# A new issue table for a linear-attention and gated-MLP kernel, and a new rule for its filler matmuls

## The chip, the cores and the metric

One Trainium2 chip, of which one core is used. The metric is the device time of one execution in microseconds; runs of the kernel before took 381.42, 377.19 and 382.31 us, median 381.42 us. A page and a trace of one profiled execution, 379.98 us long, stand behind everything that is said of the inside.

## The reference

Two parts follow each other. The first is a recurrent attention over 768 steps for 4 batches and 8 heads of width 48; its output, transposed to (4, 768, 384), is the input of the second, an MLP with a spatial gate.

```python
for t in range(S):
    cur = np.einsum('bhd,bhe->bhde', u[None] * kt, vt)
    y[:, :, t] = np.einsum('bhd,bhde->bhe', rt, state + cur)
    state = wt[:, :, :, None] * state + np.einsum('bhd,bhe->bhde', kt, vt)
...
h = np.maximum(x @ w_in, 0.0)
u, v = (h[..., :d_ff // 2], h[..., d_ff // 2:])
v_n = (v - mu) / np.sqrt(var + 1e-06)
v_s = np.einsum('ts,bsd->btd', w_spatial, v_n) + b_spatial[None, :, None]
gated = u * v_s
return (gated @ w_out).astype(np.float32)
```

## The kernel before

The sequence is cut into chunks of 128 steps, six for each batch, so that 24 *slots* (i = 0 to 23) make up the attention. In a slot, the decays W are multiplied up along time by two scans on VectorE (DVE), F and W; kk and rr (k and r) are multiplied by them on DVE or GpSimd (POOL); TensorE (PE) then forms kk times rr (tile pp, `slot_a`, L487), transposes kk (pt, `slot_kt`, L504), multiplies the transposed KT by v for the state (pp, `slot_pd`, L562), and writes the output py by four strips of 32 rows at a time (`slot_inter` and `slot_intra`, both through `mm_y` at L516). These are small matmuls of 48 or 64 rows and columns. The first six slots get their diagonal from a matmul with two columns (pg, L417), the later ones from a product N on DVE or POOL. DVE copies pp under a mask into As (L490), which `slot_intra` multiplies with v. The state goes through S0 and three tiles SA (`slot_s`).

The MLP works on the attention's output, xT, with each operand split into a high and a low part of a shorter float type; `mm3` (L614 to L616) makes one product as three matmuls. `hv_unit` makes v (ph, 128x512), `scale` normalises it into vh and vl, `g_unit` makes u (pu) and the spatial product (pv, with the spatial weights ws), both 128x384, and multiplies them into gh and gl; `out_unit` makes the output (po), which is copied to ot and stored. Weights are loaded as raw 64-bit words and unpacked on the engines (`split64`, tiles wi and wo; `prep_sp`, tile ws).

All of this is recorded as 1,757 operations (`op`), each with its engines, its cost as the planner sees it, and what it reads and writes. The order is not found while the kernel is built: the string PLAN has for each operation, in the order of recording, an engine letter (T, V, A, G, S for PE, DVE, ScalarE, POOL, SyncE) and a start time in base 36, in hundredths of a microsecond. `plan` sorts the operations by these times, and `issue` writes them in that order to the engines' queues. The times do nothing else to the real operations: each engine takes its queue in order and waits by semaphores for what it needs. All loads and stores go through SP's queue in this order too.

PE's clock has two levels. To keep it up in the first part, where PE has gaps, `fill` goes through the planned order and puts *filler* in gaps ahead of PE operations: calls of one 128x128 matmul of zeros zk into an unused part of pyw (`warm`, L854). It stops at the operation `last`, which is recorded after slot 5 (FILL_TO). In the trace each filler is two instructions, since a product of 32-bit floats is issued in two. After this the page has PE busy to the end.

Of the kernel before, what the change touches and what calls it, by code (L numbers as in the profile page):

```python
# [29 lines left out]
T19r Sdc S9l S4k6 S39x S73 Akk Vmy Vo7 Vu9 A17i G1pt Sc3 Auf Vw8 Vxh V16p A27a G29r Spa A1ek V1hp V1ka V1nn  # L30
A1po G1ut S3c S4l S5u S8c Vfg Tuv Vbj Vf0 Vh4 Vhs Aog Ghl Vl9 Axn Anx Ayb Tla Amp Tol Vq6 Grk Txe Tyf V14x
T17c T18p A1ao T1cf A1di S1f0 A1we V1zy V22k V265 A3bk G3ep Smg A162 V18e V1de V1g1 A1o0 V3lp S1xh A29v V2tt
V2v2 V2zd A36l V3p2 S3vw A4s6 V4x8 S2ic A2tg V4da S1yq A2cw G3y8 S1zz A2e2 V3u9 S450 A58r V5ch S2y9 A3fr
G40w S6e4 A6qj G7n2 S57l A5hr G5rf S6xs A7fr G7ke S218 A2gj G2lj S4vq A5bb V5gc S7wr A85w G87j S1b9 A3d0
V4el V4fo V4hb A4m1 V4o8 S2fu A2x9 V312 V324 V3jg A44m G47p S4ix A4tb V4v8 V4yj V506 A566 V57p S3l3 V3x9
V4im V4jo V4mo A532 V561 T1vz T2fn T2oz A2ro A2uw A2ye Sau Sfu Sel Skj Vz5 T11h Vr3 Vvx Vx5 V11r A159 G11a
G19k A1g0 A1a5 A1go V10u G14q T14z A18y T1at V1ch V1f3 T1gn T1ng V1pk T1s0 T1ux A1xt T1za A20e T21v T2i5
T2k2 A2q1 A2ul A2v9 Snp S10d S1a0 S1ci V1im T1kx V19b V1pc V1rd V1sm A1w3 V1lz V20v A1nq A1sb A21z V1ro G1t8
T1p5 A1r4 T1tm V1vr G1y8 T242 T253 V29i T2by T2db A2f7 T2hl A2io T2qx T2vi T2xg A332 A381 A38p A3b1 V3ch
V3c7 V3ct G3di G3ea G3i4 G3iw A3pt A3t5 V3vk A3nu A417 V45k A3lv A46t V4bm S1dr S1pe S1w8 S1tw V24h T26s  # L40
V1wr V248 V2bb V2ck A2g9 V27u G2g6 A29l A21g A2jq V2bm G2d6 T2aa A2bp T2ec V2fx V2k4 T2m9 T2na V2pf T2t4
# [71 lines left out]
Tqgf Vqh9  # L113
"""

GAP, FILL_TO = 0.8, 5

EARLY = 8

# [872 lines left out]
```

## Time and profile before

| | before |
|---|---|
| runs, median of 3 | 381.42 us (377.19 to 382.31) |
| the profiled execution | 379.98 us |
| its span, first to last instruction | 378.2 us |
| mean granted PE clock, share of full | 0.963 |
| PE matmuls busy, share of the span | 95% |
| DVE, ScalarE (ACT), POOL busy | 67%, 50%, 28% |
| matmul instructions, filler among them | 5994, 48 |

The 1.8 us between the execution's own time and its span lie around the profiled instructions. Busy time of PE is modelled at the ends of its pipelined matmuls. In the clock column 1.00 is 2.4 GHz and 0.50 is 1.2 GHz. "PE" rows are matmuls, "PEld" rows the loads of their weights, which run beside the matmul ahead. Where a wait is put down to "issue", the profile shows nothing that the engine waited for.

### The profile page before, as it was taken

What the parts mean: (1) busy time and instruction counts of PE and PEld (TensorE: products, weight loads), DVE (VectorE), ACT (ScalarE), POOL (GpSimd) and SP (SyncE); (2) the same over time, 40 slices, a digit from 0 to 9 for tenths busy, and PEclk for the clock granted to TensorE, in tenths of its full rate; (3) what the DMA queues carried; (4) which work ended last, traced back from release to release, by engine and by line L of the source; (5) the groups of instructions that cost most, each with busy time, mean ns of one, the idle gap of its engine ahead of it and who ended that gap; (6) DMA issues with size and microseconds to landing.
All of it is one profiled execution on the core that took longest, in us unless ns stands there. A gap on an engine that the chain in (4) does not pass through costs nothing.

```text
span 378.2 us, 13807 instructions
## 1 busy us (share of the span) xinstructions
PE 361.2 (95%) x5994; PEld 327.0 (86%) x5994; DVE 253.4 (67%) x491; ACT 190.4 (50%) x525; POOL 107.0 (28%) x140
## 2 busy tenths in 40 slices
PE   5799899999999999999999999999999999999995
PEld 5777678899889788999988898989989888999995
DVE  6989489999877786867577587656556754342131
ACT  2556578994456437872244138651154336722122
POOL 3505417114314242170401312144620041003111
PEclk9856599999999999999999999999999999999999
DMA  7967447673564645424233637243234420120221
GB/s 207 248 174 221 127 121 234 177 207 105 159 177 118 185 143 167 148 72 156 68 114 92 196 103 223 58 157 85 50 109 146 132 63 5 27 77 2 55 93 66
DMA packets 33023, 47.91 MB, mean 127 GB/s; under 512 B 3264, under 2 KB 21824, under 8 KB 32960
## 3 DMA queue, kind: packets, MB, share of 16 engines
q1 hardware_dynamic: 32960, 47.00, 43.0%
q8 instruction: 48, 0.79, 0.9%
q14 instruction: 15, 0.12, 0.1%
HBM read 42.27 MB, written 4.72 MB: 124 GB/s over the span
## 4 chain that ended last, share of the span: by engine, by line
PE 78%; DMA 8%; DVE 5%; ACT 4%; issue 2%; POOL 2%; SPq 1%; DVEq 0%; POOLq 0%; ACTq 0%
PE pyw L516 9%; PE pv L614 8%; PE pv L615 8%; PE pv L616 8%; PE ph L614 5%; PE ph L616 4%; PE ph L615 4%; PE pu L614 4%; PE po L614 4%; PE po L616 4%; PE po L615 4%; PE pu L615 3%; PE pu L616 3%; DMA kk<-in_tr_dram 3%; PE pp L487 3%; DMA rr<-in_tr_dram 3%
## 5 line engine op out<-in xcount | busy, mean ns | idle before, releaser
L614 PE MATMUL pv<-ws,vh 128*128 128x384 f32 x192 | 66.8, 348 | 0.0
L615 PE MATMUL pv<-ws,vh 128*128 128x384 f32 x192 | 64.9, 338 | 0.6 <-POOL ws L325 0.6
L616 PE MATMUL pv<-ws,vl 128*128 128x384 f32 x192 | 64.8, 338 | 0.0
L720 DVE TENSOR_TENSOR t<-pv,b_sb 128x384 f32<-128x384 f32 x32 | 17.7, 553 | 30.9 <-PE pv L616 30.8
L614 PEld LDWEIGHTS pv<-ws,vh 128*128 128x128 f32 x192 | 36.0, 188 | 1.3 <-ACT ws L323 0.3
L615 PEld LDWEIGHTS pv<-ws,vh 128*128 128x128 f32 x192 | 36.1, 188 | 0.9 <-POOL ws L325 0.9
L616 PEld LDWEIGHTS pv<-ws,vl 128*128 128x128 f32 x192 | 36.1, 188 | 0.0
L724 ACT CAST gh<-t 128x384 fp32r<-128x384 f32 x32 | 15.9, 512 | 38.3 <-POOL t L722 25.6
L614 PE MATMUL pu<-xT,wi 128*128 128x384 f32 x96 | 34.0, 355 | 0.0
L614 PE MATMUL po<-wo,gh 128*128 128x384 f32 x96 | 32.8, 342 | 0.0
L615 PE MATMUL pu<-xT,wi 128*128 128x384 f32 x96 | 32.4, 338 | 0.0
L432 DVE TENSOR_TENSOR_SCAN F<-W,zz 112x512 f32<-112x512 f32 x24 | 29.1, 1212 | 5.0 <-ACT zz L444 3.7
L616 PE MATMUL pu<-xT,wi 128*128 128x384 f32 x96 | 32.4, 337 | 0.0
L615 PE MATMUL po<-wo,gh 128*128 128x384 f32 x96 | 32.3, 336 | 0.0
L616 PE MATMUL po<-wo,gl 128*128 128x384 f32 x96 | 32.3, 336 | 0.0
L614 PE MATMUL ph<-wi,xT 128*128 128x512 f32 x72 | 31.5, 438 | 0.0
L582 POOL TENSOR_TENSOR SA<-S,prod 112x256 f32<-112x256 f32 x22 | 17.5, 797 | 43.9 <-DVE S L579 25.1
L616 PE MATMUL ph<-wi,xT 128*128 128x512 f32 x72 | 29.5, 409 | 0.1
L615 PE MATMUL ph<-wi,xT 128*128 128x512 f32 x72 | 29.3, 407 | 0.0
L442 DVE TENSOR_TENSOR_SCAN W<-W,zz 112x512 f32<-112x512 f32 x24 | 29.1, 1212 | 0.2
L471 ACT ACTIVATE As<-id,dg 128x64 f32<-128x64 f32 x112 | 28.3, 338 | 0.1
L600 ACT CAST xT<-pyw 128x384 fp32r<-128x384 f32 x24 | 11.5, 481 | 32.4 <-PE pyw L516 31.0
(184 smaller groups left out, 817.3 us busy)
## 6 DMA issues: line engine op xcount, KB each, us to landing
N<-in_nat_dram SPq DMA_DIRECT2D x18, 384.0 KB, 3.7
Nw<-in_gt_dram SPq DMA_DIRECT2D x16, 384.0 KB, 3.5
W<-in_tr_dram SPq DMA_DIRECT2D x24, 224.0 KB, 4.1
kk<-in_tr_dram SPq DMA_DIRECT2D x24, 224.0 KB, 3.8
rr<-in_tr_dram SPq DMA_DIRECT2D x24, 224.0 KB, 4.0
v<-in_nat_dram SPq DMA_DIRECT2D x24, 192.0 KB, 3.9
out_dram<-ot SPq DMA_DIRECT2D x24, 192.0 KB, 3.1
wst<-in_w_spT_dram SPq DMA_DIRECT2D x12, 192.0 KB, 4.5
```

The source lines that it names most:

```text
L432: op({"V": 1.22}, lambda: nc.vector.tensor_tensor_scan(flat(F())[:, ::-1], W[:, 2:][:, ::-1], flat(zz[:R])[:, ::-1], 0.0, ALU.mult, ALU.ma ...
L442: op({"V": 1.22}, lambda: nc.vector.tensor_tensor_scan(W[:, :n], W[:, :n], flat(zz[:R]), 0.0, ALU.mult, ALU.max), r=[("zz", 0)], w=[wk])
L471: e.mul(As()[:, h, :], id2, dg()[:, h:h + 1])
L487: nc.tensor.matmul(pa[ts, j, g, :], kk()[rs, g, ts], rr()[rs, g, ts], start=True, stop=True)
L516: nc.tensor.matmul(py[Q * n:Q * (n + 1), x, k_, :], a, b, start=(x, n) not in seen, stop=True, skip_group_check=True)
L582: op({"V": 0.42, "G": 0.617}, lambda e: e.tensor_tensor(new, S0, Wc.unsqueeze(2).broadcast_to([R, G, E2]), ALU.mult), r=[("S0",), ("Wc", i ...
L600: op({"A": 0.48}, lambda: nc.scalar.copy(part(hi), ps), r=[("py", 0)], w=[(hi, j)], banks=("PY",))
L614: nc.tensor.matmul(ps, ah, bh, start=first, stop=False)
L615: nc.tensor.matmul(ps, ah, bl, start=False, stop=False)
L616: nc.tensor.matmul(ps, al, bh, start=False, stop=last)
L720: op({"V": dve(HT)}, lambda: nc.vector.tensor_tensor(t1(), pv()[:, :HT], b_sb[:, tsl], ALU.add), r=[(pv, 0), ("b", 0)], w=[(t1, 0)])
L724: op({"A": act(HT)}, lambda: nc.scalar.copy(gh(), t1()), r=[(t1, 0)], w=[(gh, 0)])
```

## The change

The table PLAN is replaced as a whole; two constants and the filler's rule are new; the planner's costs of six PE operations are written anew. No operation is added or removed but filler, and an operation that may run on several engines may change its engine.

```diff
-T19r Sdc S9l S4k6 S39x S73 Akk Vmy Vo7 Vu9 A17i G1pt Sc3 Auf Vw8 Vxh V16p A27a G29r Spa A1ek V1hp V1ka V1nn
...
+T2vp S9l Sau S3tl S3cw Sjh A1ae V1e8 V1fh V1i2 A1n6 V1z1 S8c Asu Vvj Vws Vys A18y V1nj Swg A1eb V1h5 V1ko
...
-GAP, FILL_TO = 0.8, 5
+GAP, FILL_TO = 0.35, 5
+
+WINDOW, DUTY = 3.41, 0.7
...
-        op({"T": 0.32}, tp, r=[(kk, 0)], w=[(pm_, 0)])
+        op({"T": 0.36}, tp, r=[(kk, 0)], w=[(pm_, 0)])
...
-        op({"T": 0.28}, mm, r=[(rr, 0)] + [("SA", (2 * i + x) % NA) for x in range(first, 2)],
+        op({"T": 0.33}, mm, r=[(rr, 0)] + [("SA", (2 * i + x) % NA) for x in range(first, 2)],
...
-        op({"T": 0.49}, mm, r=[(As, 0), (v, 0), ("vp", i % 2)], w=[("py", 0)], mode="strips", banks=("PY",))
+        op({"T": 0.62}, mm, r=[(As, 0), (v, 0), ("vp", i % 2)], w=[("py", 0)], mode="strips", banks=("PY",))
...
-            op({"T": 0.694}, lambda k_=k_: mm3(
+            op({"T": 0.70}, lambda k_=k_: mm3(
...
-            op({"T": 0.523}, lambda k_=k_: (us(), mm3(
+            op({"T": 0.53}, lambda k_=k_: (us(), mm3(
...
     def fill(order):
-        t = first = 1.1
+        t, runs = 1.9, []
+
+        def busy(a, b):
+            return sum(max(0.0, min(e, b) - max(s, a)) for s, e in runs)
+
         for o in order:
             if o.on == "T":
-                if t < last.start and o.start - t > GAP:
-
-                    warm((o.start - t - GAP) / (0.214 if t > first else 0.43))
-                t = max(t, o.start + o.eng["T"])
+                s, took = o.start, o.eng["T"]
+                if t < last.start:
+                    n = int(min((DUTY * WINDOW - busy(s - WINDOW, s)) / 0.214 + 0.99, (s - t - GAP) / 0.214))
+                    if n > 0:
+                        warm(n)
+                        runs.append((t, t + n * 0.214))
+                runs.append((s, s + 0.85 * took))
+                t = max(t, s + took)
             yield o
```

The other two products of 128x384 go from 0.523 to 0.53 in the same way. The old rule fills every planned gap of more than 0.8 us up to 0.8 us. The new one looks, ahead of each PE operation, at the planned time just before it, counts filler in full and every other PE operation at 85% of its planned length, and puts in as many fillers as bring the share to 0.7, as far as the planned gap less 0.35 us has room. The program has 24 fillers before and 39 after.

PE's queue at its start, up to slot 1's diagonal (pg); pyw<-zk is filler, pt, pp and pg belong to slot 0 first. Before:

```order
L854 MATMUL pyw<-zk 128x128 x13
L504 MATMUL pt_188<-ident,kk_145 128x112 x4
L562 MATMUL pp<-v_151,KT_195 48x48 x16
L854 MATMUL pyw<-zk 128x128 x5
L417 MATMUL pg_232<-up_sb,rk_163 128x2 x4
L516 MATMUL pyw<-rr_147,SA_126 32x64 x8
L487 MATMUL pp<-rr_147,kk_145 64x64 x16
L417 MATMUL pg_282<-up_sb,rk_276 128x2 x4
```

After:

```order
L856 MATMUL pyw<-zk 128x128 x12
L506 MATMUL pt_186<-ident,kk_147 128x112 x4
L419 MATMUL pg_193<-up_sb,rk_166 128x2 x4
L856 MATMUL pyw<-zk 128x128 x2
L564 MATMUL pp<-v_156,KT_198 48x48 x16
L856 MATMUL pyw<-zk 128x128 x6
L518 MATMUL pyw<-rr_145,SA_126 32x64 x8
L489 MATMUL pp<-rr_145,kk_147 64x64 x16
L419 MATMUL pg_276<-up_sb,rk_242 128x2 x4
```

Slot 0's diagonal pg goes ahead of the state product, and there are two groups of filler after it instead of one ahead of it.

PE's queue right behind this, from slot 1's transpose to the first strips of slot 1 (rr_160 before, rr_154 after). Before:

```order
L504 MATMUL pt_290<-ident,kk_165 128x112 x4
L516 MATMUL pyw<-As_251,vp_121 32x64 x16
L516 MATMUL pyw<-As_251,v_151 32x64 x16
L516 MATMUL pyw<-rr_147,SA_126 32x64 x8
L854 MATMUL pyw<-zk 128x128
L562 MATMUL pp<-v_170,KT_341 48x48 x16
L604 MATMUL pyw<-xT_0_0_350,nident 128x192 x2
L854 MATMUL pyw<-zk 128x128 x2
L516 MATMUL pyw<-rr_160,SA_125 32x64
```

After:

```order
L506 MATMUL pt_290<-ident,kk_160 128x112 x4
L518 MATMUL pyw<-As_230,vp_121 32x64 x16
L518 MATMUL pyw<-As_230,v_156 32x64 x16
L518 MATMUL pyw<-rr_145,SA_126 32x64 x8
L856 MATMUL pyw<-zk 128x128 x2
L564 MATMUL pp<-v_206,KT_334 48x48 x16
L606 MATMUL pyw<-xT_0_0_350,nident 128x192 x2
L856 MATMUL pyw<-zk 128x128 x8
L518 MATMUL pyw<-rr_154,SA_125 32x64
```

The real work stands in the same order; there are 2 and 8 fillers where there were 1 and 2. Behind the pp matmuls of slot 1 the new queue has another 6 ahead of its As matmuls, where the old one has 2 ahead of slot 2's pg.

SP's queue around the load of kk for slot 17 (kk17; the number behind a name is the slot's, W0 and W1 are the two tiles of W, out_0_dram a store of the output). Before:

```order
L380 DMA W1_116<-in_tr_dram 112x4x128
L387 DMA N17_3460<-in_nat_dram 128x768
L384 DMA rr16_3468<-in_tr_dram 112x512
L380 DMA W0_115<-in_tr_dram 112x4x128
L742 DMA out_0_dram<-ot0_1_2_2722 128x384
L384 DMA kk17_3566<-in_tr_dram 112x512
L388 DMA v17_3571<-in_nat_dram 128x384
```

After:

```order
L382 DMA W1_116<-in_tr_dram 112x4x128
L399 DMA Nw9_3456<-in_gt_dram 128x768
L386 DMA kk17_3464<-in_tr_dram 112x512
L386 DMA rr16_3470<-in_tr_dram 112x512
L744 DMA out_0_dram<-ot1_0_2_3549 128x384
L386 DMA rr17_3560<-in_tr_dram 112x512
L382 DMA W0_115<-in_tr_dram 112x4x128
```

kk17 has moved ahead of rr16, of the load of W0 and of the store that stood just before it.

## Rows read from the trace of the kernel before

**Rows 1.** The page's busy us (share of the span) and instructions of each engine

```profile
span 378.2 us, 13807 instructions
...
PE 361.2 (95%) x5994; PEld 327.0 (86%) x5994; DVE 253.4 (67%) x491; ACT 190.4 (50%) x525; POOL 107.0 (28%) x140
```

**Rows 2.** Stretches: length, busy us of each engine (instructions), granted clock, DMA share, GB/s

```profile
0.00:16.00 16.00, 10.09 (x133) 9.24 (x134) 12.55 (x27) 5.92 (x17) 5.87 (x21) 1.00 0.89 229
16.00:33.00 17.00, 16.43 (x342) 13.84 (x343) 14.88 (x23) 8.78 (x26) 7.29 (x7) 0.50 0.63 170
33.00:36.40 3.40, 3.11 (x76) 2.13 (x75) 3.40 (x7) 3.27 (x13) 0.30 (x2) 0.99 1.00 297
36.40:46.60 10.20, 8.43 (x164) 6.41 (x172) 5.39 (x10) 5.53 (x19) 5.31 (x5) 0.50 0.57 166
46.60:77.00 30.40, 29.21 (x672) 24.36 (x657) 27.82 (x54) 25.70 (x70) 9.92 (x10) 1.00 0.63 177
77.00:378.00 301.00, 293.90 (x4633) 271.00 (x4631) 189.38 (x375) 141.23 (x385) 78.34 (x98) 1.00 0.38 111
```

**Rows 3.** PE's waits up to 47 us: releaser, us in total, times, longest

```profile
PE pyw L854 <- DVE pyw L269: 1.9, 1, 1.9
PE pyw L516 <- issue: 1.7, 1, 1.7
PE pt L504 <- POOL kk L445: 1.6, 1, 1.6
PE pg L417 <- DVE e_('wv', 0)_172 L352: 1.3, 1, 1.3
...
PE pt L504 <- ACT dg L459: 0.3, 1, 0.3
```

**Rows 4.** Timeline of PE: like work at half and full clock (start, us, instructions)

```profile
10.13 1.38 PE L854 MATMUL pyw<-zk 128*128 128x128 f32 x10
...
23.81 1.22 PE L854 MATMUL pyw<-zk 128*128 128x128 f32 x4
...
26.46 1.14 PE L487 MATMUL pp<-rr,kk 48*64 48x64 f32 x32
27.52 1.01 PE L504 MATMUL pt<-ident,kk 112*128 112x112 f32 x4
...
31.65 0.63 PE L615 MATMUL ph<-wi,xT 128*128 128x512 f32 x1
...
46.81 0.69 PE L487 MATMUL pp<-rr,kk 48*64 48x64 f32 x32
...
47.77 0.39 PE L615 MATMUL ph<-wi,xT 128*128 128x512 f32 x1
...
51.98 0.55 PE L504 MATMUL pt<-ident,kk 112*128 112x112 f32 x4
```

**Rows 5.** Waits of PE's weight loads from 77 us on

```profile
PEld pyw L516 <- issue: 5.9, 22, 0.4
PEld pyw L516 <- DVE As L490: 2.3, 4, 1.0
...
PEld pv L615 <- POOL ws L325: 0.9, 1, 0.9
...
PEld pp L562 <- DVE vl L686: 0.3, 1, 0.3
```

**Rows 6.** The chain that ended last, around slot 17's kk (start, us, what)

```profile
209.48 0.84 SPq L742
...
210.44 4.45 DMA kk<-in_tr_dram
...
214.91 0.70 DVE kk L445
...
215.75 0.57 PE pt L504 x4
```

More of the change, by code (lines that the diff above doesn't have):

```diff
@@ new lines @@
+T2xr V312 T34b T361 A38c T3bq A3do T3g9 T3i7 T3k5 A3pl A3rl A3s9 S24g S2gj S2nu S2va G308 T3cg V2pc V2zr
+V32u V343 A3d8 G340 V37l A3gd A3u8 A3ka V336 G3ff T38s A3c1 T3ey V3ic V3lh T3p7 T3qe V3t7 T3wg T3y6 A40j
+T43m A45x T4j0 T4ky T4mw A4rc A4td A4u0 S2u1 S2zp S37h S3bn V3jt T3mp V3f7 V3mf V3vy V3wk A425 V3nz V44k
+A3r8 A41l G47f V3uz V411 T3s4 A3vx T3zd V43n V469 T48u T4a1 V4cu T4g3 T4ht A4mr T4ou A4qa T4sf T4ud T4wb
+A4zu A51u A52i A54v V557 V56d V56z V57j G58k G59c G5a3 A5hp A5k1 V5m9 A5lg A5nt V5ts V5b3 A5d0 V5ws Ta7o
@@ new lines @@
+S3ph A43c S46a A4k6 S4n3 A4x9 S507 A5a8 T3un T426 T4d7 A4gi T5l4 T5ml T5o2 T5pj T65y T67f V6bm V6d9 A6nr
+V72k T446 T45n T474 A4bo T69g T6ax T6u7 T6vo T743 T76k V79y G7c2 A7mo G7on T4qy T517 T545 A58p T5f8 T5gp
+T5r0 T5sh T5ww T61b V63n V7jl A7lj G7rb T3t3 T40o T4bq A4p8 T5i6 T5jn T5ty T5vf T5yd T5zu V64y V6ek A78m
+V7kv T7z0 T80h T81y T84f V87g Sb77 T7t4 T7ul T7w2 T7xj A7zw S8cu T8fx T8he T8m1 T8ni A8vb Sa3f T4y9 T4zq
+T52o A5eg T6y5 T78l T7a2 T7bj T7d0 T7in V7r4 V837 A8n2 G97d T6i8 T6jp T6l6 A6ow T9ac T9nt T9pa T9t8 T9up
@@ new lines @@
+T9w6 Va7q Va9d Aaje Vam5 T6ps T6r9 T6sr A6v2 T8te T8uv T91r T938 T98v T9ez V9hc Va2y Aa4y Vanh T5at T5ca
+T5dr A5gn T8xc T8yt T90a T9gg T9hx T9je V9qc V9wt Aa2v Ga4u Tas7 Tato Tav5 Tawm Aazt Sbva Tay4 Tazl Tb12
+Tb87 Abaj Sbgd Tbcu Tbeb Tbfs Tblp Abo0 Sdtw S3ae S3sc S3zm S5d6 S40v V477 V4ao V4em V4fa A4jl V4aw V4jx
+V5nx V5pk V5r8 A5rs A5t5 T4eo V4if T4pn V4sp V4ty T56w T582 V5z5 T631 T64r A66o T68w A6ab T6ce T6ec T6ga
+A6j3 A6l4 A6lr S47j S4bz S4oc S5ss S4qu V4na V4sg V4zb V57s A5p8 V4qr V6h6 G62y G660 V69f A6w4 A6bd V4zn
@@ new lines @@
+V55f T55m A57i T59i V5do G6be T6mw T6o3 V6tz T6zv T71l A75j T781 A79s T7k4 T7m2 T7o0 A7s3 A7u3 A8o7 S5gx
+S5a0 S667 S6b0 S6ra V66a V6js V6kd V6l0 A6py G6s6 V6yz G6me G6pg V6sq A7au A707 V6iv G6kt T6x5 A6z0 T72s
+V76i V77r T7er T7fx V7m7 T7q8 T7ry A7ud V7wj T8a3 T8c1 T8dz A8ie A8kf A8l2 A8r9 V8s3 V8wa V8ww V8zl V955
+G966 G96x V9ay A9vb V9y5 A97x A9zv Gadz Vasj Abcf Vc0w S6ji S6q1 S7kt S6ua S72j V6vt V72c V7j9 V7nz A7rs
+V70n V81i V757 G7eq V7hz A8g0 G7u0 V791 G7hf T75k A77f T7hc V7sg G7wr T866 T87c V8ad T8j4 T8ku A8q6 V8xd
@@ new lines @@
+Tacl Tahh Tajf Aam8 Aao8 Aaow S71a S7hv S7tp S7jk S7sh V7td V8c5 V8dn V8ea A8i4 V7zu V8hs V84i V865 V88s
+A8gj A8ap V7yw V8cq T83f A85b T88t V8u4 V8vd T94y T965 V995 T9c3 T9dt A9fl V9vj Ta1u Ta3s Ta5q Aa8j Aaak
+Aab7 S8bl S8e3 S99c S8ac S8rr V8oy V8x5 V8zu V90h A9gn V8sf V9rn V8ke V8m2 V8no A9zb V9in V8yo G90e T8wc
+V93n T97k V9tc V9ul T9xx T9z3 Va4a Ta87 Ta9x Aad7 Vafg Tald Taob Taq9 Aat2 Aav2 Aavq Aay3 Gb1v Vb0d Gb1g
+Gb2n Gb3f Gb47 Vb56 Abp2 Abs4 Vbwb Vbxz Abzx Vc4p Vb5q Ab7o Vbjz S8p9 A8za S928 A9ca S9fk A9wq S9zo Aae9
@@ new lines @@
+Tab4 Taej Tag0 Aaic Tc2m Tc43 Tcbo Tcd5 Tcem Tcg3 Vckt Vcmg Adlx Vdt8 T9kv T9mc T9qr Aa1t Tchk Tcj1 Tcwa
+Tcxr Tcz8 Td1p Vdc7 Gdkf Ae0t Ve4d T8oz T8qg T8rx A8u9 Tcng Tcox Tcqe Tcrv Tctc Tcuu Vcx6 Gdbz Adpl Ve32
+Tbh9 Tbiq Tbk7 Abmj Tbq3 Tbrk Tc5k Tc71 Tcki Tclz Vcvq Gd44 Ad7c Gd9c Tekz Temg Teny Tepe Aerr Sf4c Teag
+Teqv Tesc Tett Aew6 Sfnd Tebx Tegk Tei1 Teji Aem7 Senx Tb6q Tbn5 Tbom Abr1 Tdk9 Tdno Tdp5 Tdui Tdxx Tdze
+Ve1q Gf1b Agai Ggch Tbu2 Tbvi Tbwz Ac1c Tff7 Tfgo Tfto Tg19 Tg2q Tg47 Vg6k Vgzs Ahhr Vhk6 Te0v Te2c Te4t
@@ new lines @@
+Ae97 Tewr Tezp Tf16 Tf2n Tf44 Tf5l Vf7y Vf9l Afq6 Vgyg Tgj3 Tgkk Tgm1 Agoe Teva Tey8 Tf72 Tfo9 Tfpq Tfr7
+Vgca Vgqc Ah0t Ghbp Thyt Ti0a Ti1r Ti38 Ai5l Sj5p Thoi Thvv Thxc Ti4p Vi9z Sk99 Thpz Thrg Thsx Thue Ailo
+Sixs S8qi S983 Sa4o Sah6 S9eb V9ka V9pg V9q1 V9zt Aaa6 V9ns Vayp Var8 Vatt Vavg Aa1a Vax2 T9s8 A9u4 Ta0j
+Vaao Gace Tb2t Tb3z Vb70 Tb9x Tbbn Abdu Vbml Td36 Td9b Tdb9 Ade2 Adg3 Adn2 Sa0x Sa26 Sb2a Sax1 Saag Vagr
+Valx Vaos Vb0n Abc5 Vak8 Gbd0 Gb78 Gbaa Vbdk Abbl Vbun Vaek Vap3 Tanb Aaym Tb5f Vblo Gbnd Tbyp Tbzw Vc2w
@@ new lines @@
+Tc8s Tcai Acfo Vcjj Tdd7 Tdf5 Tdlq Adqq Adsr Adtk Sb11 Sb5y Scch Sbf4 Sbhm Vbet Vc2l Vcax Vcbk Acfe Vbib
+Gd0p Vbp6 Vbqt Vbsg Gd00 Vbz9 Vbtq Vcpp Tbt1 Abuw Tc1b Vcqy Gcso Td5e Td6k Vddi Tdhc Tdj2 Adkv Vdmm Tdqm
+Tdsk Tdvz Ae1y Ae3z Ae4m Aea9 Veeb Vecj Ved5 Veev Vefg Veg0 Geh1 Vfgs Ag0e Gg5p Afrc Aftp Vfw1 Ahix Ahtq
+Ghwh Sbwj Sc1u Sbxs Sbu1 Scdq Vcgd Vcns Vcyh Vcz4 Ad8i Vco0 Gdn3 Vc6d Vc80 Vc9o Adp2 Acgq Vcut Vduj Td0q
+Vd3j Td80 Vdvs Gdxi Te6j Te7q Veaq Tedo Tefe Aeh6 Vetn Tfzb Tg8u Tgas Agdm Agfm Agga Sd54 Sdku Sec2 Scb8
@@ new lines @@
+Sdjl Vdnx Vdsc Vdsw Vdwq Ae0j Vdzv Veps Gcu9 Gcxb Vd2a Adt1 Gf3z Ve5o Ge7e Te3t Ve6l Te95 Vedd Verg Tf9t
+Tfaz Vfez Tfjv Tfll Afne Vfp5 Tgh5 Tgtc Tgva Agyv Ah1y Ah2l Sdv5 Seat Sep6 Sd3v Sf33 Veg8 Vejq Veka Veky
+Aeor Veo3 Gexw Gden Gdhp Vdr2 Ag1u Afv3 Vesq Vfe2 Tf8j Afaf Tfcf Vfqg Vfrp Tfve Tfwl Vg14 Tg5y Tg7o Ag9g
+Vgkz Tgni Tgpg Tgre Agu8 Agw8 Agww Ah4y Ghed Vham Vhb8 Ghf5 Vhg4 Ghh5 Ghhx Vi2v Ai6n Viin Ahkw Ahql Ght2
+Vhiw Ahs0 Vi0b Sdsn Ae6m Se9k Aejl Setc Af4w Sf7u Afih Th0d Th1u Th3b Ah5o Tiyk Tj01 Tj8v Tjac Tjbt Tjda
@@ new lines @@
+Vjfm Vjh9 Ajl6 Gjn4 Tiad Tifq Tij5 Aimq Tj1i Tj2z Tj4g Tj5x Tj7e Tjn2 Vjq1 Vkcb Akea Gkg9 Tgcq Tge7 Tgfo
+Agi9 Tjin Tjk4 Tjll Tjoj Tjzl Tk12 Vk3f Vk52 Ak71 Gkki Tfdq Tfi5 Tfms Afp4 Tins Tip9 Tiqq Tis7 Tito Tiv5
+Viz2 Gj16 Aj4e Vjud Tkza Tl1r Tl94 Tlf2 Vlhf Sljd Tkos Tkq9 Tkrq Tkt7 Akvk Sln4 Tkxt Tl38 Tl4p Tl66 Vl8j
+Slzk Them Thg3 Thhk Ahmv Tk2j Tk40 Tk8n Tka4 Tkbl Tkd2 Vkhp Glaw Almw Vmcr Th7q Th97 Thc5 Ahgp Tlgj Tlky
+Tlmf Tlnw Tlpd Tlqu Vm16 Vm2t Amf7 Vn5i Th4s Th69 Thao Ahd1 Tlsb Tlwq Tly7 Tlzo Tm15 Tm43 Vm6n Vm8a Ambh
@@ new lines @@
+Vmgt Tjv6 Tjwn Tjy4 Ak86 Tm5k Tm81 Tmmp Tmu9 Tmvq Tmx7 Vmzj Gn1n An4v Gn71 Tnpa Tnqr Tns8 Tntp Ao0e So25
+Tnje Tnkv Tnmc Tnnt Anq5 Sou9 Tnv6 Tnwo Tny4 Tnzl Ao1x Sovi Ses3 Sfcy Sfzs Sfom Sfm4 Vfaw Vfmx Vfsn Vg7v
+Agbo Vfl8 Vggr Gfzy Gg2z Vgb0 Agbz Vgif Tfso Vfuj Tfy0 Vfzx Vgm9 Tgxi Tgyo Vh13 Thjb Thl1 Ahv5 Vi44 Tibu
+Tids Tih7 Aik0 Aipg Aiq3 Sf1u Sfyj Sg94 Sgkc Sh1w Vgdl Vgk3 Vgkn Vgn7 Ah0i Vgsl Vh2v Vgvi Vgx5 Vhgc Ai82
+Gidj Vgrn Vhlh Thdm Ahfi Thm7 Vho4 Vhpe Ti6g Ti7m Vigu Tikv Timl Aioe Viq5 Tiwm Tjer Tjgp Ajji Ajmb Ajmy
```

115 lines of the change are left out of this document (30 added, 85 removed).

## The prediction

> **What bounds the kernel now.** I read the page's busy table first [rows 1]. TensorE's matmuls cover 361.2 of 378.2 us, so all its waits together are 17.0 us; the next engine, DVE, is busy for 253.4 us. TensorE is the bound, and no change of order takes work from it. The Trainium skill (Trainium Kernel Development and Optimization, section Performance Expectations) calls matmul busy time a bad metric and weight loads a good one; by the weight loads, busy 327.0 us [rows 1], 51.2 us would be open instead of 17.0. My sum stays under both.
>
> The second view is the table of stretches [rows 2]. From 77 us on, PE is busy 293.9 of 301.0 us at full clock. Before 77 us it is another kernel: the granted clock is 0.50 from 16.0 to 33.0 and from 36.4 to 46.6 us, which is 1.2 of 2.4 GHz for 27.2 us, and PE is busy 16.43 and 8.43 us of these two. That is work at half speed, not waiting. In the same 17.0 us DVE is busy 14.88 us, so a faster PE would soon stand behind DVE there; from 36.4 to 46.6 no other engine is busy more than 5.53 of 10.2 us.
>
> The third view is who PE waited for. Up to 47 us it waits 8.6 us in eight rows [rows 3]: 1.9 ahead of the first filler, 1.7 for nothing that the profile shows, and 5.0 for other engines. From 77 us on I take its weight loads, which stop first [rows 5]: five rows of "issue" sum to 8.2 us and six rows with an engine's name to 4.5 us, the longest for As (2.3) and ws (0.9). The 8.2 us belong to the same strips in any order. Only the 4.5 us can be reordered away.
>
> **The change part by part.** The table sets only the order of instructions on each engine; nothing on the chip waits for its times. So "longer hand-over times" cost nothing by themselves, and the new figures for PE work (0.53 for 0.523 and the like) remove no matmul: both kernels do the same 5,946 real ones. Three terms are left.
>
> *Term 1, the clock before 47 us.* Like work at half and full clock [rows 4]: 32 strips of pp take 1.14 and 0.69 us, four transposes 1.01 and 0.55, one 128x512 matmul 0.63 and 0.39. The ratio is 1.62 to 1.84; I take 1.65. The 24.9 us that PE is busy at half clock [rows 2] would be 15.1 us at full clock: 9.8 us is the most that the clock can give back. The least is nothing. Between them stands DVE: it leaves 17.0 - 14.88 = 2.1 us in the first stretch, and in the second PE's share alone limits, 8.43 - 8.43/1.65 = 3.3 us; the 1.7 us without a named releaser lie in that stretch too and stay. That makes 5.4 us, and I take 5.5, near the middle.
>
> Why should the clock come back? Before it rises at 33 us PE has just run three 128x512 matmuls; the strips, the two-column pg and the transposes that fill 16 to 31 us did not raise it, although they kept PE busy. Filler is full 128x128 matmuls, so it is like the first kind. The old rule set 23 fillers ahead of the third transpose, the new one 36 (12, 2, 6, 2, 8, 6 against 13, 5, 1, 2, 2): eight and six of them now stand in slot 1, where the strips were. I expect the half clock to last about half as long, not to vanish: between the first filler and the first transpose PE still waits for the kk load.
>
> *Term 2, the filler's own price.* 13 more fillers there. Ten instructions (five fillers) take 1.38 us at full clock, 0.28 each; four (two fillers) 1.22 us at half clock, 0.61 each [rows 4]. So 13 x 0.28 = 3.6 us or 13 x 0.61 = 7.9 us on PE's queue. The cover is the 5.0 us that PE waits there for others [rows 3]. At full clock they hide and cost 0; at half clock 7.9 - 5.0 = 2.9 us stand out; with no cover at all it is 7.9. A filler stands ahead of slot 1's strips, the next pp and As matmuls in PE's queue, so DVE's copy of pp into As and POOL's and DVE's state update wait behind it. I take 0, since the 36 are sized for gaps and the clock is mostly up.
>
> *Term 3, order after 77 us.* The waits that end in PE begin with a load. The chain at 209 us shows it [rows 6]: kk of slot 17 is issued at 210.44 behind an output store on SP, lands 4.45 us later, DVE multiplies at once, and the transpose starts at 215.75. In the new SP order that load stands ahead of rr of slot 16, a W load and the stores, where it stood behind all of them; by the table's own figures the lead from a load's issue to its first use grows from a median of 5.0 to 5.8 us. The gain is between 0 and 4.5 us; a new order can also open waits that the old one did not have, which I bound by the same 4.5 us on the other side. Nearest to the row of slot 17, where the wait clearly goes, I take 2.5 us: DVE and POOL have 37% and 74% of this stretch free [rows 2], so little stands behind the load.
>
> The tail stays: the last output matmul, its copy and store close both programs. Nor do I price the first 16 us: W, rr and kk of slot 0 are still the first three loads; kk's product moves little, and slot 0's rr product goes from DVE to POOL beside it.
>
> Sum against the profiled execution: 379.98 - 5.5 + 0 - 2.5 = 372.0 us. The median of the runs shown is 381.42, 1.4 us more, so this is 2.5% under the median. What a measurement of this kernel can tell from no change is about 2%: below 373.8 or above 389.0 us.
>
> **The rivals.** *The filler does not hold the clock.* The half clock lasts as long as before and only term 3 is left: 379.98 - 2.5 = 377.5 us. For it: PE was busy 16.43 of 17.0 us and had the half clock all the same [rows 2], and the new rule counts every planned matmul, strips and two-column ones too, as 85% busy, so it may stop filling too soon. Against it: 13 more full matmuls in just that stretch. A rule of the Trainium skill bears on it (TensorE: Matmul & The Clock Gate, Part 1, What's actually happening): the clock is set by how busy PE has recently been. Read by the busy row, PE was busy enough already and filler would change nothing, which gives this rival's 377.5; the trace disagrees with that reading, since 97% busy went with half clock.
>
> *DVE is next.* The clock comes back, but DVE, busy 64.0 of the first 77 us [rows 2], holds the chain in both stretches, and only 2.1 us of term 1 remain: 379.98 - 2.1 - 2.5 = 375.4 us. For it: DVE's share of 14.88 in 17.0. Against it: in the second stretch DVE is half idle.
>
> *Filler at half clock stands in the way: slower.* The eight and six fillers come up while the clock is still 0.50, each takes 0.61 us, the strips and the As matmuls behind them start late, and slots 1 and 2 shift on DVE as well. Price 2.9 us over the cover, and new waits eat term 3: 379.98 + 2.9 = 382.9 us. It decides from the point where the fillers' time passes the 5.0 us of waits, at 0.38 us for each of the 13. Against it: fourteen full matmuls in slot 1 are what should raise the clock.
>
> *Everything gives.* All of term 1 and term 3: 379.98 - 9.8 - 4.5 = 365.7 us.
>
> **How the numbers follow.** Forecast 0.52; everything 0.11; clock not held 0.18; DVE next 0.11; slower 0.08. The forecast's own range is 368 to 376 us, about four fifths of it below 373.8. Faster by over 2%: 0.42 + 0.11 = 0.53 and 0.01 from the edge of DVE next, 0.54. Slower by over 2% needs fillers with no cover (7.9) and new waits of 4.5 us besides, 392 us: half of the slower rival, 0.04. Within 2%: 0.42. The range runs from the end of "everything", 365, to just under the slower rival, 381.
>
> **What would show it.** Right: the granted clock is 0.50 for 8 to 18 us before 60 us instead of 27.2; the filler's groups show 24, 4, 12, 4, 16 and 12 instructions, those in slot 1 nearer 0.28 than 0.61 us for each two; PE reaches its dense stretch 4 to 7 us earlier; from there on PE's weight loads wait under 2.5 us for named engines and still about 8 us for "issue". Wrong: half clock for 25 us or more (clock not held); PE waiting for DVE's As, S or kk for over 6 us before 77 us (DVE next); filler groups at 0.6 us each with PE never idle around them (slower); or over 5 us of named waits after 77 us, which would mean that the new order starves PE where the old one did not.

## The result and the profile after

The changed kernel takes 375.74 us (median of 20 runs, 372.86 to 378.08); the kernel before, run beside it, 379.9 us. The ratio is 0.9884 with a 95% interval of 0.9857 to 0.991: 1.2% faster, under the 2% bound of the prediction though clear of no change, and about half of the gain that was forecast (372.0 us). The profiled execution took 372.86 us, the fastest of the 20, so its profile flatters the change a little; three repeats follow below. Each ratio in this document counts only the runs within 1.5% of their kernel's fastest, while medians and ranges count all runs.

The page of the kernel after, in the columns of [rows 1]:

```profile
span 370.5 us, 13876 instructions
...
PE 357.3 (96%) x6024; PEld 326.0 (88%) x6024; DVE 255.8 (69%) x498; ACT 183.8 (50%) x504; POOL 108.1 (29%) x140
```

PE is busy 3.9 us less although it has 30 more instructions, all of them filler: its clock is higher. The stretches, in the columns of [rows 2]:

```profile
0.00:16.00 16.00, 12.41 (x135) 11.35 (x135) 11.47 (x26) 6.10 (x18) 6.37 (x22) 0.89 0.89 224
16.00:33.00 17.00, 15.56 (x372) 13.52 (x372) 14.77 (x28) 10.68 (x34) 7.30 (x5) 0.90 0.69 202
33.00:46.60 13.60, 11.35 (x383) 8.92 (x383) 13.57 (x23) 10.20 (x31) 7.73 (x6) 1.00 0.73 212
46.60:60.00 13.40, 12.77 (x267) 11.32 (x268) 13.15 (x26) 12.56 (x40) 4.88 (x8) 1.00 0.75 214
60.00:77.00 17.00, 16.57 (x339) 14.30 (x338) 16.76 (x36) 14.97 (x37) 3.38 (x5) 1.00 0.68 185
77.00:370.50 293.50, 288.59 (x4534) 266.63 (x4532) 186.12 (x365) 129.29 (x349) 78.41 (x96) 1.00 0.37 109
```

The clock column is where the change shows: half clock is left only from 10.84 to 14.25 and from 21.08 to 24.49 us (the clock's records), 6.8 us instead of 27.2. Both figures leave out the start: the records begin at 7.42 us here and at 5.64 us in the kernel before, and ahead of them the view prints 1.00, although the first line of the timeline below has the opening fillers at 0.46 us each, as long as at half clock. Counted with that time, PE was at half clock for 14.2 us instead of 32.9. The third column behind the length is new too: DVE is busy 13.57, 13.15 and 16.76 us from 33 to 77 us, 43.5 of 44.0. PE's waits up to 47 us, which answer to [rows 3]:

```profile
PE pyw L856 <- DVE pyw L271: 1.9, 1, 1.9
PE pyw L518 <- POOL rk L414: 1.5, 1, 1.5
PE pt L506 <- POOL kk L447: 0.9, 1, 0.9
...
PE pyw L518 <- DVE As L492: 0.5, 1, 0.5
```

The 1.7 us of "issue" are gone in this execution. Four filler groups in the timeline, to be held against [rows 4]:

```profile
1.86 5.49 PE L856 MATMUL pyw<-zk 128*128 128x128 f32 x24 [1.86 <-DVE pyw L271]
...
12.27 2.53 PE L856 MATMUL pyw<-zk 128*128 128x128 f32 x12
...
21.12 3.65 PE L856 MATMUL pyw<-zk 128*128 128x128 f32 x16 [0.65 <-ACT xT L609]
...
25.71 1.60 PE L856 MATMUL pyw<-zk 128*128 128x128 f32 x12
```

Two instructions are one filler: 0.46, 0.42, 0.46 and 0.27 us each. Last, the waits of PE's weight loads from 77 us on, as in [rows 5]:

```profile
PEld pyw L518 <- issue: 6.7, 25, 0.4
PEld pyw L890 <- DVE okr L886: 1.0, 1, 1.0
PEld pyw L518 <- DVE xT L611: 0.7, 1, 0.7
PEld pyw L518 <- ACT zz L446: 0.4, 1, 0.4
```

As and ws, the two largest of before, are no longer there, and slot 17's transpose does not wait for its kk. All rows with a name make 4.0 us, of which 1.0 is the range check at the very end.

**One measure for all runs.** Fixed times cut the work at different places. I therefore summed the planned lengths of PE's real operations (the new table's lengths, for every kernel) in the order of its queue and took from the trace when 40 us of them were done (*t40*, near 75 us) and when 318 us were (close to the end). "Real", "filler" and "idle" are PE's busy time in the two kinds of matmul and the rest up to t40, summed from the trace (overlaps at the pipelined ends count in both kinds: 0.2 to 1.4 us, and 2.3 with more filler). "Later" is from 40 to 318 us of work. "Half" is the half clock on record before t40. It leaves out the first 5.3 to 8.1 us, which have no record, except without filler, where all 36.9 us come from the lengths of the matmuls.

| profile | t40 | real | filler | idle | half | later |
|---|---|---|---|---|---|---|
| before | 75.4 | 56.6 | 9.6 | 9.7 | 27.3 | 295.2 |
| before, repeat | 76.4 | 55.8 | 11.2 | 10.0 | 27.3 | 294.0 |
| after | 71.5 | 48.3 | 15.8 | 8.3 | 6.8 | 291.2 |
| after, repeats 1 to 3 | 73.1, 75.9, 71.7 | 50.4, 51.5, 49.6 | 14.4, 15.0, 14.2 | 9.3, 10.4, 8.9 | 10.2, 13.7, 6.8 | 290.5, 292.1, 292.0 |
| new table, old filler rule | 71.9 | 50.8 | 12.2 | 9.6 | 10.2 | 290.7 |
| old table, new filler rule | 76.4 | 52.3 | 14.5 | 11.0 | 20.5 | 294.8 |
| new table, no filler | 74.4 | 57.4 | 0.4 | 16.8 | 36.9 | 292.0 |
| new table, more filler | 77.9 | 50.2 | 19.3 | 10.7 | 6.8 | 292.4 |
| new table, DVE relieved | 73.1 | 50.4 | 14.3 | 9.3 | 10.2 | 290.9 |
| old table, loads earlier | 76.6 | 57.8 | 11.1 | 8.3 | 30.7 | 292.2 |
| new table, loads later | 72.1 | 51.3 | 14.3 | 7.5 | 10.2 | 293.7 |
| new table, old rule, loads earlier | 72.6 | 52.6 | 12.4 | 8.2 | 17.1 | 291.4 |

On average the four profiles with the changed kernel reach t40 2.9 us sooner than the two of before (73.0 for 75.9) and need 3.2 us less for the later part (291.4 for 294.6). Those four lie 4.4 us apart in t40 but only 1.6 us in the later part, so a single t40 tells little. The row with more filler comes from a run of 380.41 us of a kernel whose runs begin at 373.27 us, and decides nothing.

### The profile page after: what moved, and what is told of

It reads as the page before. It is cut to its first block, busy times and chain, and to the rows that moved or that the text cites. A ratio compares the mean times of both kernels' runs of the same rounds, so it can differ in the third digit from the quotient of the medians.

```text
span 370.5 us, 13876 instructions
## 1 busy us (share of the span) xinstructions
PE 357.3 (96%) x6024; PEld 326.0 (88%) x6024; DVE 255.8 (69%) x498; ACT 183.8 (50%) x504; POOL 108.1 (29%) x140
## 4 chain that ended last, share of the span: by engine, by line
PE 88%; DVE 4%; DMA 3%; ACT 2%; issue 1%; SPq 1%; ACTq 0%; DVEq 0%
PE pv L616 10%; PE pyw L518 9%; PE pv L617 9%; PE pv L618 9%; PE pu L616 5%; PE ph L616 5%; PE po L616 4%; PE pu L617 4%; PE pu L618 4%; PE ph L618 4%; PE ph L617 4%; PE po L618 4%; PE po L617 4%; PE pp L489 4%; PE pt L506 2%; PE pyw L856 2%
## 5 line engine op out<-in xcount | busy, mean ns | idle before, releaser
L726 ACT CAST gh<-t 128x384 fp32r<-128x384 f32 x32 | 16.2, 511 | 46.5 <-DVE t L724 24.7
L584 POOL TENSOR_TENSOR SA<-S,prod 112x256 f32<-112x256 f32 x18 | 13.8, 767 | 59.5 <-DVE S L581 22.9
L616 PE MATMUL ph<-wi,xT 128*128 128x512 f32 x72 | 30.0, 416 | 0.0
L492 DVE COPY_PREDICATED As<-mask,pp 128x512 f32<-128x512 int32 x24 | 17.8, 740 | 17.0 <-PE pp L489 10.6
L618 PE MATMUL ph<-wi,xT 128*128 128x512 f32 x72 | 28.4, 395 | 0.0
L617 PE MATMUL ph<-wi,xT 128*128 128x512 f32 x72 | 28.4, 394 | 0.0
L713 ACT ACTIVATE us<-pu 128x384 f32<-128x384 f32 x32 | 15.6, 489 | 25.1 <-PE pu L618 25.0
```

The lines of the kernel that those rows point to most:

```text
L492: op({"V": 0.73}, lambda: nc.vector.copy_predicated(As().rearrange("p (g j) t -> p j g t", j=2), mask.unsqueeze(1).unsqueeze(1).broadcast_ ...
L584: op({"V": 0.42, "G": 0.617}, lambda e: e.tensor_tensor(new, S0, Wc.unsqueeze(2).broadcast_to([R, G, E2]), ALU.mult), r=[("S0",), ("Wc", i ...
L616: nc.tensor.matmul(ps, ah, bh, start=first, stop=False)
L617: nc.tensor.matmul(ps, ah, bl, start=False, stop=False)
L618: nc.tensor.matmul(ps, al, bh, start=False, stop=last)
L713: op({"A": act(HT, True)}, lambda: nc.scalar.activation(us(), pu()[:, :HT], AF.Relu), r=[(pu, 0)], w=[(us, 0)])
```

## The experiments

**Which part of the change brings the gain?** The first run keeps the new table and takes the old `fill` and GAP back (34 fillers); the second is the reverse (also 34). The edit of the first, cut to its core:

```diff
-GAP, FILL_TO = 0.35, 5
+GAP, FILL_TO = 0.8, 5
...
-                    n = int(min((DUTY * WINDOW - busy(s - WINDOW, s)) / 0.214 + 0.99, (s - t - GAP) / 0.214))
...
+                if t < last.start and o.start - t > GAP:
+                    warm((o.start - t - GAP) / (0.214 if t > first else 0.43))
```

> The new table with the old filler rule (gaps of more than 0.8 us filled up to 0.8 us), which sets 34 fillers there in four groups: 18, 4, 6 and 4, against 12, 2, 6, 2, 8, 6 and one of the changed kernel. Theory F (the filler rule holds the clock, and that is most of the gain): half the clock's gain goes, 377 to 379 us, and the granted clock is 0.50 for 15 us or more. Theory T (the new table brings the gain, and the filler rule as such almost nothing): 375 to 376.5 us, as the changed kernel.

> The old table and costs with the new filler rule, 34 fillers instead of 24 (12, 2, 7, 1, 4, 4, 1, 1). Theory F: 376 to 378 us, with the half clock under 18 us. Theory T: 379 to 381 us, no change from the kernel before.

Measured: 374.89 us, ratio 0.985 [0.9812, 0.9888], for the new table with the old rule; 381.83 us, 1.0046 [1.0007, 1.0084], for the old table with the new rule. The new table with either rule has the whole gain, and the new rule by itself has none: theory T holds, though both times fall just outside its ranges (0.1 us below, 0.8 us above). The same number of fillers gave 10.2 us of half clock and t40 at 71.9 us with one table, 20.5 us and 76.4 us with the other. What this does not show is that filler in slot 1 is of no use: on the new table the old rule too puts ten fillers there, six of them in this group.

```profile
20.06 2.93 PE L856 MATMUL pyw<-zk 128*128 128x128 f32 x12 [1.36 <-ACT xT L609]
```

**How much filler?** The rule is switched off, or made to fill more.

```diff
-WINDOW, DUTY = 3.41, 0.7
+WINDOW, DUTY = 3.41, -1.0
```

```diff
-GAP, FILL_TO = 0.35, 5
+GAP, FILL_TO = 0.05, 5
...
-WINDOW, DUTY = 3.41, 0.7
+WINDOW, DUTY = 3.41, 1.1
```

> The changed kernel with no filler but the two single ones that are operations of their own. Theory F: half clock for most of the first 40 us, the first stretch 4 us or more later, 379 to 381 us. Theory T: the clock is lower for long too, but DVE, busy almost without a pause from 33 us on in the changed kernel, takes up most of the loss: 375 to 377.5 us.

> The changed kernel with more filler: a share of 1.1 instead of 0.7 and 0.05 instead of 0.35 us left free of a gap, 60 fillers instead of 39. Theory F: hardly any half clock after the first 8 us and 372 to 374.5 us. Theory T: the clock rises in the same way, but the time stays at 375 to 376.5 us, since DVE is next. If fillers stand in the way of real work instead: over 377 us.

Measured: 377.79 us, 0.9943 [0.9903, 0.9983], without filler, between the ranges of the two theories; 378.84 us, 0.9882 [0.9803, 0.9961], with 60, whose six runs lie from 373.27 to 385.2 us: unclear, and none of the three theories is settled by it. A timeline of PE without filler shows how to read its clock, which has no record before 36.9 us (the page prints full clock there):

```profile
36.29 0.63 PE L617 MATMUL ph<-wi,xT 128*128 128x512 f32 x1
...
39.05 0.58 PE L506 MATMUL pt<-ident,kk 112*128 112x112 f32 x4
```

The 128x512 matmul takes the 0.63 us of half clock [rows 4]; behind the first record four transposes take 0.58, as at full clock. From its first matmul at 7.96 us on, its work up to 36.9 us has the lengths of half clock. That is 22.7 us more than after, counted alike (14.2 us), and it reached t40 only 1.4 us later than the mean of the four profiles of after. Its profile is 1.4 us shorter than its median, though; by the medians filler is worth 2.1 us (377.79 to 375.74).

**How far do profiles of one kernel differ?** Kernels with no edit at all: the changed one three times, the one before once.

> The changed kernel once more, unchanged, for a second profile: its first one was the shortest of twenty runs (372.86 us; their median is 375.74). Theory L (the first profile was lucky in PE's stalls without a named releaser): a run near 375.7 us has 4 to 7 us of them before 77 us instead of 0.8, and the work done by 77 us is 3 to 4 us later. Theory C (the clock differs from run to run): the half clock lasts 13 us or more and the stalls stay under 2 us.

> The same again, with the same expectations: theory L 4 to 7 us of stalls without a releaser before 77 us in a run near 375.7 us; theory C 13 us or more of half clock.

> The same again, with the same expectations: theory L 4 to 7 us of stalls without a releaser before 77 us in a run near 375.7 us; theory C 13 us or more of half clock.

> The kernel before once more, unchanged. Both theories: 379 to 381 us, 4 to 8 us of stalls without a releaser before 77 us, and the same named waits of about 4.5 us after 77 us, since those come from the order. If the waits after 77 us differ by more than 1.5 us, the third term cannot be read from single profiles.

Measured: 373.38, 378.23 and 373.80 us; 379.79 us. With after's first profile, PE's weight loads wait 0.8, 2.5, 5.7 and 2.8 us for "issue" before 77 us, and the times go with it: 372.86, 373.38, 378.23, 373.80. The second repeat also has the longest half clock (13.7 us), so that theories L and C both fit it; none of the three repeats came near 375.7 us. The named waits of the weight loads after 77 us differ as well: without the range check at the end they sum to 3.0, 3.8, 3.8 and 5.1 us in the changed kernel, and to 4.5 and 4.9 in the two profiles of the kernel before. They can't carry the third term. The longest stall of these four profiles is in the second repeat:

```profile
PEld pyw L518 <- issue: 3.4, 4, 2.4
```

The 2.4 us stand from 36.87 to 39.30 us, and the clock falls to half at 37.96. What these stalls are is told at the end.

**Is DVE the bound from 33 to 77 us?** In the changed kernel, seven subtractions of the weight unpacking that DVE runs there go to POOL, by letters of the table.

```diff
+        for n in (75, 78, 84, 87, 90, 108, 139):
+            assert self.ops[n].on == "V"
+            self.ops[n].on = "G"
         return sorted(self.ops, key=lambda o: o.start)
```

> The changed kernel with seven subtractions of the weight unpacking (five of ws and wo at 0.55 us, two of wi and wo at 0.55 to 0.68), which DVE runs between 42 and 77 us, given to POOL; nothing else moves. Theory D, DVE is the bound from 33 to 77 us (43.5 of 44.0 us busy): DVE gets 4 us back there, its busy time in the stretch falls below 42 us, PE does the same work 1.5 to 3 us earlier at 77 us, and the ratio to the kernel before is 0.978 to 0.985. Rival P, POOL's tensor operations hold DVE's back (in the changed kernel's trace eight DVE operations that run beside a POOL one take 6.1 us longer than their like before 77 us): with seven more of them the extra time of DVE grows by 2 us or more, and the ratio is 0.986 to 0.992, no gain over the changed kernel.

Measured: 375.61 us, ratio 0.9895 [0.9853, 0.9937]. The stretch from 33 to 77 us, columns of [rows 2], and who DVE waits for in it:

```profile
33.00:77.00 44.00, 39.43 (x911) 32.88 (x911) 39.14 (x68) 35.03 (x98) 21.31 (x25) 0.92 0.63 182
```

```profile
DVE S L584 <- PE pp L567: 2.3, 2, 1.9
...
DVE As L495 <- PE pp L492: 0.8, 1, 0.8
```

DVE is busy 39.1 us instead of 43.5, and now waits for PE, where in the changed kernel it waited for nobody. The room on DVE was made and no time came of it: the interval of the ratio begins at 0.9853, just above the 0.978 to 0.985 of theory D. The profile alone would not show this: its t40 of 73.1 us is the mean of the four profiles of after, but its weight loads wait 6.0 us for "issue" before 77 us (one stall of 2.7 us at 34.06), more than any of those. Rival P was right about the ratio, and its extra time of DVE grew by 1.2 us (6.1 to 7.3), less than its 2.

**Do the loads' leads make the later part?** First the kernel before, with loads after 70 us moved up SP's queue by up to 2 us, as far as the planned release of the buffer allows; then the changed kernel with them 1 us later.

```diff
+            if o.on == "S" and o.start > 70 and o.fn.__qualname__.find("out_unit") < 0:
+                t = max([o.start - 2.0] + [p.start + p.eng[p.on] for p in o.pre])
...
+                if t < o.start:
+                    o.start = t
```

```diff
+            if o.on == "S" and o in use and o.start > 70:
+                o.start = max(o.start, min(o.start + 1.0, use[o] - 0.3))
```

The planned times only sort SP's queue, so what the chip gets is another order. In the first kernel a load passes a store of the output 13 times and another load 38 times; in the second the loads keep their order and a store passes a load 20 times.

> The kernel before, with each load after 70 us planned up to 2 us earlier in SP's queue, as far as the planned release of its buffer allows (0.75 us on average; two in five by 1 us or more); all other engines keep the old order. Theory L, the new table's gain after 75 us comes from the loads' longer lead: the later part of the work (from the point where 40 us of PE's planned operations are done to that where 318 are; 295.2 and 294.0 us in two profiles of the kernel before, 290.5 to 292.4 with the new table) takes 291 to 293 us, ratio 0.992 to 0.996. Rival O, it comes from the order of the computing engines: the later part stays at 294 to 295 us, ratio 0.998 to 1.003.

> The changed kernel with every load after 70 us planned 1.0 us later in SP's queue (the median planned lead from issue to first use falls from 5.8 to 4.8 us, less than the old table's 5.0); all else is the changed kernel. Theory L: named waits of PE's weight loads after 77 us rise from 3 to 6 us or more, the later part takes 293.5 to 296 us, ratio 0.994 to 1.000. Rival O: named waits stay near 3 us, the later part at 290.5 to 292.4 us, ratio 0.986 to 0.991.

Measured: loads earlier in the old table 377.96 us, 0.9974 [0.9942, 1.0005], later part 292.2 us; loads later in the new table 379.2 us, 0.9936 [0.9893, 0.9979], later part 293.7 us. The later part went where theory L put it, both times, in one profile each. The idle time of PE's weight loads in it says the same: 26.0 and 24.7 us in the two profiles of before, 22.8 with earlier loads; 21.9 to 23.5 with the new table, 25.1 with later loads. The whole times are less sharp. The first ratio lies between the ranges of L and O and its interval includes no change; in its profile t40 is late (76.6 us, 30.7 us of half clock), a part that the edit does not touch. The second ratio misses L's range by 0.0004 and its interval overlaps the changed kernel's. And named waits of the weight loads, without the tail's 1.0, are 4.8 us, where L expected 6; the third repeat has 5.1 with no edit. The largest of them:

```profile
PEld pt L513 <- ACT st L654: 0.7, 1, 0.7
PEld pv L623 <- DVE t L729: 0.6, 1, 0.6
PEld pp L571 <- DVE KT L517: 0.5, 1, 0.5
```

No row there names a load. The waits of PE's matmuls after 77 us are sharper than those of its weight loads, part of which the matmul ahead covers. Before, all rows with an engine's name:

```profile
PE pyw L516 <- DVE As L490: 1.1, 2, 0.7
PE pv L615 <- POOL ws L325: 0.6, 1, 0.6
PE pt L504 <- DVE kk L445: 0.6, 1, 0.6
PE pp L562 <- DVE t L720: 0.5, 1, 0.5
```

That is 2.8 us, and 2.1 in the repeat of before and in the old table with the new filler rule. With the loads earlier it is 0.7. The changed kernel's four profiles have 0.2 to 1.1 without the range check, and with the loads later it is 1.7, now with a load as the largest:

```profile
PE pp L571 <- DMA v<-in_nat_dram: 0.8, 1, 0.8
```

So the order of loads and stores moves the waits of PE in both directions, as theory L has it.

**A better version?** The new table with the old filler rule and loads up to 2 us earlier.

> The new table with the filler rule of the kernel before (as in the run with the old rule, ratio 0.985), and each load after 70 us planned up to 2 us earlier, as far as its buffer's planned release allows (0.83 us on average; the median planned lead from issue to first use grows from 5.9 to 7.1 us, the leads under 3.5 us fall from 8 to 2; the kernel before has 5.0 us and 20). Theory L, the lead of loads still limits the part after 75 us: the later part of the work (from 40 to 318 us of PE's planned operations; 290.5 to 292.4 us with the new table) takes 289 to 290.5 us and the ratio to the kernel before is 0.979 to 0.983, below both kernels. Rival E, the new table's leads are already enough: the later part stays at 290.5 to 292.4 us and the ratio at 0.984 to 0.988.

Measured: 375.46 us, 0.9861 [0.9809, 0.9912], later part 291.4 us. Rival E held: the new table's leads are enough. In the planned order of before, 20 loads with a first use after 75 us have a lead under 3.5 us, in the new one 8, here 2; the step from 20 to 8 paid, from 8 to 2 it did not. The count of short leads is not the whole measure, though: the old table with earlier loads still has 16 of them, with a median lead of 5.9 us, and had most of the gain. No version is shown to beat the changed kernel; the best median, 374.89 us with the old rule, has an interval that overlaps its own.

## Why the prediction was half right

**Term 1 (−5.5 us, the clock) and term 2 (0, the filler's price) have to be read together.** The clock came back about as far as argued: 6.8 to 13.7 us of half clock on record where 8 to 18 was forecast. The gross gift lies close to the 9.8 us named as the most: real matmuls up to t40 take 48.3 us for 56.6, 8.3 less. The step that failed is term 2's "I take 0, since the 36 are sized for gaps". PE's filler time grew by 6.2 us (9.6 to 15.8) while its idle time fell by 1.4 only: 4.8 us were not hidden (3.8 on the mean of the profiles), well inside the 0 to 7.9 that was bounded and far from the value taken. The fillers were priced at 0.28 us each, as if the clock were up; the 36 ahead of the third transpose took 14.9 us, where the 23 of before took 9.6, so 0.41 for each of the 13 more, because groups of twelve, six and eight ran while the clock was low (0.42 to 0.46 each). The 0.61 us that was read for half clock was too much as well: a group of two counts its modelled ends most. Net, t40 is 3.9 us sooner in this profile and 2.9 on the mean, short of the 4 to 7 us that were forecast for the dense stretch.

**What made the clock rise was named rightly, but the new rule is not what puts it there.** I gave the rise to fillers in slot 1, and the records go with their number between slot 1's transpose and the third one: with none the clock rises at 36.9 us, with the 5 of before at 32.9 (repeat 33.6), with 9 (old table, new rule) at 26.8, with 10 (new table, old rule) at 23.8 and 26.1, with 16 at 24.5; in the three repeats of after it rose by 17.5 us and then stayed up through slot 1. On the new table the old rule does as well as the new, since its planned gaps lie there. The new rule on the old table took 6.8 us off the half clock and gave 4.3 us on real matmuls, and its own filler (+4.9) and idle time (+1.3) ate all of it. Which rows of the new table make the early part shorter was not taken apart; that it does not need the new filler rule is shown. Nor is the clock shown to be all of it: the profile without filler reached t40 1.5 us sooner than before with 4 us more of half clock, a step that is inside the spread of t40.

**"Clock not held" and "slower" fall, one of them narrowly.** Half clock did not stay. The point from which "slower" was to decide, 0.38 us for each of the 13 fillers, was passed (0.41), and the kernel was faster all the same: that rival's sum left out that the same fillers give the clock back.

**"DVE is next" is the nearest rival (375.4 us) and right in its picture, not in its cause.** DVE did fill up, to 43.5 of 44.0 us. But the sign set for it, PE waiting over 6 us for DVE's As, S or kk, is not there (0.5 us for As and 0.4 for kk up to 77 us), and relieving DVE by 4.4 us gained nothing measurable. A busy engine with nobody waiting for it is no bound; DVE seems to have run ahead with weight unpacking. The early part looks like a chain through PE, ACT, DVE and POOL in turn, in which 8 us less on one engine come back as filler and idle time; that picture fits the table, no run proves it.

**Term 3 (−2.5 us, loads) was right in cause and near in size, the size in part by luck.** It is 3.2 us on the mean, and moving the loads alone takes 2.4 us off the old table's 294.6 and puts 2.3 us on the new table's 291.4. The reading of [rows 6] was the good one: a load behind a store of the output. But the 2.5 us were taken out of the 4.5 us of named waits of the weight loads, and these hardly fell (3.0 to 5.1 us in four profiles, where under 2.5 was forecast). One repeat even passed the 5 us that were to mean that the new order starves PE, with a later part of 292.0 us. The gain sits in many small gaps of the weight loads and shows best in the waits of the matmuls.

**The sum.** −5.5 + 0 − 2.5 = −8.0 was forecast; −2.9 − 3.2 = −6.1 is the mean of the profiles, 374.6 us on the mean of four profiled executions, and the median of 20 runs is 375.74. "The tail stays" was not quite so: the rest of the execution, behind 318 us of work and around the span, is 0.7 us longer, so the means of the profiled executions differ by 5.3 us. The medians of 20 runs differ by 4.2. The weight of 0.54 on "faster by over 2%" rested on the term that was cut in half.

## What to carry to other kernels

Price filler by what it takes at the clock at which it will run, and set it against the idle time that it can really replace: more clock on the busiest engine is worth only what the chain behind it can use. Look first for loads that stand behind a store in a queue that is taken in order, and stop when more lead no longer pays; a late load mostly hides behind the name of the engine that read it, and the waits of the matmuls show it better than those of the weight loads. And profile one kernel several times before explaining 1%: four profiles of one program differed by 5.4 us.

## What the runs showed of the hardware

**PE stands where its instruction stream arrives.** The stalls of PE that the profile calls "issue" and that last over 1.1 us before 77 us all stand among the strips or the small pp matmuls. The trace holds the 48 packets of the larger of two queues named "instruction" (0.79 MB in all). Stall and last packet landed ahead of its end, in us (read from the packets' records):

```
before          38.22 to 40.08   packet 37.51 to 38.75   lands 1.34 ahead
before, repeat  38.85 to 40.96   packet 38.44 to 39.69   1.27
after, repeat 2 36.87 to 39.30   packet 36.77 to 37.80   1.49
after, repeat 3 34.63 to 36.86   packet 34.59 to 35.54   1.32
DVE relieved    34.06 to 36.73   packet 34.33 to 35.44   1.29
more filler     66.97 to 69.85   packet 67.36 to 68.61   1.24
```

Each time PE goes on 1.2 to 1.5 us after the packet has landed. So it is in 17 of the 20 stalls over 1.1 us before 77 us in all 14 profiles (1.2 to 1.7 us); without filler, three of 1.2 to 1.6 us (up to 25.64 us) have no packet that lands within 5 us ahead of their end. The strips use up instructions fastest (32 in 0.27 us from 27.24 us on in the changed kernel), and the six stand where the DMA share is near 0.6 to 0.7. They read as PE waiting for its own program; no edit that changes the fetch alone was tried, so this stays an inference. These stalls go with much of what differs between executions, and the clock can fall in them.

**DVE and POOL hold each other up.** Two operations on 8 columns (L438), 0.17 us by the median of their like, end with POOL's operation beside them:

```profile
43.43 1.26 DVE L438 SCALAR_TENSOR_TENSOR prod<-F,W 112x8 f32<-112x8 f32 x1
```

```profile
41.63 3.03 POOL L447 TENSOR_TENSOR kk<-kk,F 112x512 f32<-112x512 f32 x1
```

POOL's ends at 44.66, DVE's at 44.69, and POOL's own 3.03 us compare with 1.28 for a product of that shape alone, so POOL seems to have waited first, behind the DVE operations ahead. The second pair is plainer: POOL's operation starts at 61.53 us and ends at 62.83 after its usual 1.29 us, DVE's starts at 61.57 and ends at 62.86. Before 77 us eight such DVE operations run 6.1 us over their median in the changed kernel, so part of "DVE busy 43.5 us" is waiting. The Trainium skill (SBUF — State Buffer, section SBUF: two separate sides) says that DVE and GpSimd share one pair of ports, and that of a GpSimd operation and a DVE operation with two inputs in SBUF, whichever starts first holds it for its whole instruction; both pairs, with ends 0.03 us apart, agree with that. A busy figure of DVE beside a busy POOL is thus an upper bound on its work.
